# Linear attention and a squared-ReLU FFN: emitting each batch's attention beside the FFN block before it, with weights in memory of their own

One core of a Trainium2 chip. The metric is the device time of one execution in microseconds (us), the median of several runs; lower is better.

## The reference, cut to what matters

```python
# q, k, v: [8 batches, 8 heads, 576 rows, 64], float32
kv  = einsum('bhsd,bhse->bhde', k, v)
out = einsum('bhsd,bhde->bhse', q, kv)
rms = sqrt(mean(out * out, axis=-1, keepdims=True) + 1e-06)
x   = (out / rms * g_norm)  -> tokens [4608, 512]
h   = maximum(x @ w_in, 0.0)          # w_in  [512, 2048]
y   = h * h @ w_out                   # w_out [2048, 512]
```

Attention of a batch gives 576 tokens. The FFN runs over blocks of 512 tokens, nine of them. So FFN block i needs attention batches 0 to i, and none later.

## The kernel before

The whole of attention comes first, in pools that are then released; then the weights are loaded into pools that take over that memory; then the FFN runs, in pools that take over the memory of the load buffers. Matmuls are in bf16. A scheduler orders the instructions of each engine when the kernel is built; on the chip each engine takes them in that fixed order.

```python
    def attention():
        apool = ctx.enter_context(tc.tile_pool(name="attn_sb", bufs=6))
        ppool = ctx.enter_context(tc.tile_pool(name="attn_ps", bufs=1, space=PSUM))
        for b in range(B):
            kv_ps_list = [ppool.tile([P, P], dt, tag=f"kv_ps{p}") for p in range(NP)]   # 4 banks
            for ci, (ss, sl) in enumerate(s_chunks):       # 5 chunks: 4 of 128 rows, 1 of 64
                # ... load kkf, vvf; cast to kk (ScalarE), vv (VectorE)
                for p in range(NP):
                    nc.tensor.matmul(kv_ps_list[p], lhsT=kpair, rhs=vpair, ...)
            # ... kv_sb = kv_ps * block-diagonal mask (VectorE)
            for ci, (ss, sl) in enumerate(s_chunks):
                # ... load qqf, cast qq; 4 transposes qT_ps, copy qT (VectorE), 4 matmuls o_ps
                # ... sq = o_ps^2 (ScalarE), sum ss (VectorE), sqrt (ScalarE), 1/x and o_sb (VectorE)
                # ... 4 transposes oT_ps, xT = oT_ps * g (VectorE)
    # ... attention(), its pools released
    wpool = ctx.enter_context(tc.tile_pool(name="w", bufs=1))
    with tc.tile_pool(name="w_tmp", bufs=2) as wtmp:
        # 4 loads of w_in, 16 of w_out, each cast to bf16 by VectorE
    fpool  = ctx.enter_context(tc.tile_pool(name="ffn_sb", bufs=2))
    fppool = ctx.enter_context(tc.tile_pool(name="ffn_ps", bufs=4, space=PSUM))
    for t0 in range(0, n_tokens, T):                       # T = 512
        for nf in range(FC):
            # 4 matmuls into hps; h2 = relu(hps) (ScalarE); h2 = h2 * h2 (VectorE)
        for mt in range(T // P):
            # 16 matmuls into yps; ysb = yps (VectorE); store
```

Of the kernel before, what the change touches and what calls it, by code (L numbers as in the profile page):

```python
# [12 lines left out]
def kernel(  # L13
# [10 lines left out]
    nc = tc.nc  # L24
    P = 128
    B, H, S, D = q.shape
    d_model = H * D
    n_tokens = B * S
    d_ff = moe_w_in.shape[1]
    KC = d_model // P  # L30
    FC = d_ff // P
    dt = mybir.dt.float32
    AF = mybir.ActivationFunctionType
    ALU = mybir.AluOpType

    s_chunks = []
    s0 = 0
    while s0 < S:
        sl = min(P, S - s0)
# [2 lines left out]

    bf = mybir.dt.bfloat16
    HPP = P // D

    const = ctx.enter_context(tc.tile_pool(name="const", bufs=1))
    identity = const.tile([P, P], dt)
    make_identity(nc, identity)
    identity_bf = const.tile([P, P], bf)
    nc.vector.tensor_copy(out=identity_bf, in_=identity)  # L50
    bdm = const.tile([P, P], dt)
# [3 lines left out]
    g_perm = const.tile([P, 1], dt)  # L55
    g_part_ap = bass.AP(tensor=g_norm.tensor, offset=g_norm.offset,
                        ap=[[int(g_norm.ap[0][0]), D], [0, 1]])
    nc.sync.dma_start(out=g_perm[:D, :], in_=g_part_ap)
    nc.sync.dma_start(out=g_perm[D:, :], in_=g_part_ap)
    eps_sb = const.tile([P, 1], dt)  # L60
    nc.vector.memset(eps_sb, 1e-6)

    xT = const.tile([P, KC, n_tokens], bf)

    def attention():
        apool = ctx.enter_context(tc.tile_pool(name="attn_sb", bufs=6))
        ppool = ctx.enter_context(tc.tile_pool(name="attn_ps", bufs=1, space=bass.MemoryType.PSUM))
        NP = H // HPP
        ns = len(s_chunks)
        for b in range(B):  # L70
            kv_ps_list = [ppool.tile([P, P], dt, tag=f"kv_ps{p}", name=f"kv_ps{p}")
                          for p in range(NP)]
            for ci, (ss, sl) in enumerate(s_chunks):
                kkf = apool.tile([P, H, D], dt, tag="kkf")
                vvf = apool.tile([P, H, D], dt, tag="vvf")
                nc.sync.dma_start(out=kkf[:sl], in_=k[b, :, ss:ss + sl, :].rearrange("h s d -> s h d"))  # L76
                nc.sync.dma_start(out=vvf[:sl], in_=v[b, :, ss:ss + sl, :].rearrange("h s d -> s h d"))  # L77
                kk = apool.tile([P, H, D], bf, tag="kk")
                vv = apool.tile([P, H, D], bf, tag="vv")
                nc.scalar.activation(out=kk[:sl], in_=kkf[:sl], func=AF.Copy)  # L80
                nc.vector.tensor_copy(out=vv[:sl], in_=vvf[:sl])  # L81
                for p in range(NP):
                    kpair = kk[:sl, p * HPP:(p + 1) * HPP, :].rearrange("s h d -> s (h d)")
                    vpair = vv[:sl, p * HPP:(p + 1) * HPP, :].rearrange("s h d -> s (h d)")
                    nc.tensor.matmul(kv_ps_list[p], lhsT=kpair, rhs=vpair,  # L85
                                     start=(ci == 0), stop=(ci == ns - 1))
            kv_sb = apool.tile([P, NP, P], bf, tag="kv_sb")
            for p in range(NP):
                nc.vector.tensor_mul(out=kv_sb[:, p, :], in0=kv_ps_list[p], in1=bdm)

            for ci, (ss, sl) in enumerate(s_chunks):
                qqf = apool.tile([P, H, D], dt, tag="qqf")
                nc.sync.dma_start(out=qqf[:sl], in_=q[b, :, ss:ss + sl, :].rearrange("h s d -> s h d"))
                qq = apool.tile([P, H, D], bf, tag="qq")
                nc.scalar.activation(out=qq[:sl], in_=qqf[:sl], func=AF.Copy)  # L95
                o_ps = ppool.tile([P, NP, P], dt, tag="o_ps", bufs=2)
                qT_ps = ppool.tile([P, NP, P], bf, tag="qT_ps")
                for p in range(NP):
                    qpair = qq[:sl, p * HPP:(p + 1) * HPP, :].rearrange("s h d -> s (h d)")
                    nc.tensor.transpose(qT_ps[:, p, :sl], qpair, identity_bf[:sl, :sl])  # L100
                qT = apool.tile([P, NP, P], bf, tag="qT")
                nc.vector.tensor_copy(out=qT[:, :, :sl], in_=qT_ps[:, :, :sl])  # L102
                for p in range(NP):
                    nc.tensor.matmul(o_ps[:sl, p, :], lhsT=qT[:, p, :sl],  # L104
                                     rhs=kv_sb[:, p, :], start=True, stop=True)

                o_sb = apool.tile([P, NP, P], bf, tag="o_sb")
                sq = apool.tile([P, H, D], dt, tag="sqsb")
                ss_ = apool.tile([P, H], dt, tag="ss")
                nc.scalar.activation(out=sq[:sl], in_=o_ps[:sl], func=AF.Square)  # L110
                nc.vector.tensor_reduce(out=ss_[:sl], in_=sq[:sl],
                                        axis=mybir.AxisListType.X, op=ALU.add)
                nc.scalar.activation(out=ss_[:sl], in_=ss_[:sl], func=AF.Sqrt,
                                     scale=1.0 / D, bias=eps_sb[:sl])
                nc.vector.reciprocal(out=ss_[:sl], in_=ss_[:sl])
                sslice = ss_[:sl]
                rstd_bc = bass.AP(tensor=sslice.tensor, offset=sslice.offset,
                                  ap=[list(sslice.ap[0]), list(sslice.ap[1]), [0, D]])
                nc.vector.tensor_mul(out=o_sb[:sl], in0=o_ps[:sl], in1=rstd_bc)  # L119

                oT_ps = ppool.tile([P, NP, P], bf, tag="oT_ps")
                for p in range(NP):
                    nc.tensor.transpose(oT_ps[:, p, :sl], o_sb[:sl, p, :], identity_bf[:sl, :sl])  # L123
                nc.vector.tensor_scalar(  # L124
                    out=xT[:, :, b * S + ss: b * S + ss + sl],
                    in0=oT_ps[:, :, :sl], scalar1=g_perm, scalar2=None, op0=ALU.mult)

    with ExitStack() as actx:
        oc = ctx
        ctx = actx  # L130
        attention()
        ctx = oc

    wpool = ctx.enter_context(tc.tile_pool(name="w", bufs=1))
    w_in_sb = wpool.tile([P, KC, d_ff], bf)
    w_out_sb = wpool.tile([P, FC, d_model], bf)
    with tc.tile_pool(name="w_tmp", bufs=2) as wtmp:
        for kk in range(KC):
            t_in = wtmp.tile([P, d_ff], dt, tag="win")
            nc.sync.dma_start(out=t_in, in_=moe_w_in.rearrange(  # L140
                "(kc ki) n -> ki kc n", ki=P)[:, kk, :])
            nc.vector.tensor_copy(out=w_in_sb[:, kk, :], in_=t_in)
        for kk in range(FC):
            t_out = wtmp.tile([P, d_model], dt, tag="wout")
            nc.sync.dma_start(out=t_out, in_=moe_w_out.rearrange(
                "(fc fi) n -> fi fc n", fi=P)[:, kk, :])
            nc.vector.tensor_copy(out=w_out_sb[:, kk, :], in_=t_out)  # L147

    T = 512
    fpool = ctx.enter_context(tc.tile_pool(name="ffn_sb", bufs=2))  # L150
    fppool = ctx.enter_context(tc.tile_pool(name="ffn_ps", bufs=4, space=bass.MemoryType.PSUM))

    for t0 in range(0, n_tokens, T):
        h2 = fpool.tile([P, FC, T], bf, tag="h2")
        for nf in range(FC):
            hps = fppool.tile([P, T], dt, tag="hps")
            for kk in range(KC):
                nc.tensor.matmul(hps,  # L158
                                 lhsT=w_in_sb[:, kk, nf * P:(nf + 1) * P],
                                 rhs=xT[:, kk, t0:t0 + T],  # L160
                                 start=(kk == 0), stop=(kk == KC - 1))
            nc.scalar.activation(out=h2[:, nf, :], in_=hps, func=AF.Relu)  # L162
            nc.vector.tensor_mul(out=h2[:, nf, :], in0=h2[:, nf, :], in1=h2[:, nf, :])  # L163

        for mt in range(T // P):
            yps = fppool.tile([P, d_model], dt, tag="yps")
            for kk in range(FC):
                nc.tensor.matmul(yps,  # L168
                                 lhsT=h2[:, kk, mt * P:(mt + 1) * P],
                                 rhs=w_out_sb[:, kk, :],  # L170
                                 start=(kk == 0), stop=(kk == FC - 1))
            ysb = fpool.tile([P, d_model], dt, tag="ysb")
            nc.vector.tensor_copy(out=ysb, in_=yps)  # L173
            nc.sync.dma_start(out=out[t0 + mt * P: t0 + (mt + 1) * P, :], in_=ysb)


# [28 lines left out]
```

## Time and profile before

| | before |
|---|---|
| time | 445.55 us (444.17 to 446.51, 5 runs); 445.41 over all 16 runs |
| attention, until the first w_in load | 153.4 us |
| weights, until TensorE runs freely | 39.2 us |
| FFN | 248.0 us |
| TensorE / VectorE / ScalarE busy | 76 / 46 / 38% of the span |

The windows, chain and waits that tell the three stages apart stand in the prediction. Here is the strip of the page, 40 slices of 11.1 us each, a digit for tenths busy (DMA is the mean over the core's 16 DMA engines):

```profile
PE   1356656656566342069999999999999999999996
DMA  8999999999999185510201102011010110101101
```

DMA is full for the first 13 slices (attention), loads the weights in the next five and then does little; TensorE is half idle for 17 and then full. The two strips are complementary, and that is what the change is after.

Three rows of the instruction groups matter later (count, total busy us, mean ns of one; then the idle time ahead of them and its cause). These are three of the four kinds of attention matmul, each 128 columns wide:

```profile
L85 PE MATMUL kv_ps<-vv,kk 128*128 128x128 bf16 (+1 forms) x160 | 22.1, 301 | 30.4 <-DVE vv L81 30.3
L104 PE MATMUL o_ps<-kv_sb,qT 128*128 128x128 bf16 (+1 forms) x160 | 24.9, 311 | 8.3 <-DVE qT L102 8.3
L123 PE MATMUL oT_ps<-identity_bf,o_sb 128*128 128x128 bf16 (+1 forms) x160 | 22.6, 293 | 21.6 <-DVE o_sb L119 21.3
```

### The profile page before, as it was taken

The numbers are of one execution on the slowest core, as the hardware profiler recorded it, in microseconds if no ns is written. First come the engines' busy times: TensorE is split into PE (matmuls) and PEld (weight loads), VectorE is DVE, ScalarE is ACT, GpSimd is POOL, SyncE is SP. The second block draws the span as 40 slices with busy tenths as digits, with TensorE's granted clock in tenths as the row PEclk, the third lists the DMA queues.
The fourth block names the chain that finished last, engine by engine and source line by source line (L and its number), as shares of the span: only waits on it lengthen the run. The fifth ranks groups of instructions, "written<-read, shape, count | busy, mean of one in ns | idle before, by whom it ended". The sixth has DMA issues, their size and how long they took to land.

```text
span 444.4 us, 4875 instructions
## 1 busy us (share of the span) xinstructions
PE 338.8 (76%) x1792; PEld 173.3 (39%) x1792; DVE 205.0 (46%) x474; ACT 167.7 (38%) x306; POOL 1.1 (0%) x9
## 2 busy tenths in 40 slices
PE   1356656656566342069999999999999999999996
PEld 0244444444344210024444444444444444444442
DVE  0387786786777633233242332423324243242431
ACT  2465565565456300044160431604316053160530
POOL 0000000000000000000000000000000000000000
PEclk9999999999999999999999999999999999999999
DMA  8999999999999185510201102011010110101101
GB/s 154 205 210 205 203 209 205 208 204 200 200 214 144 32 364 170 150 39 9 87 0 49 47 20 76 0 49 47 25 71 0 49 48 25 71 0 49 47 25 71
DMA packets 120759, 46.45 MB, mean 105 GB/s; under 512 B 113568, under 2 KB 113568, under 8 KB 120224
## 3 DMA queue, kind: packets, MB, share of 16 engines
q1 hardware_dynamic: 120736, 46.15, 48.2%
q8 instruction: 14, 0.23, 0.2%
q14 instruction: 9, 0.07, 0.1%
HBM read 36.70 MB, written 9.44 MB: 104 GB/s over the span
## 4 chain that ended last, share of the span: by engine, by line
PE 65%; DMA 14%; DVE 12%; ACT 3%; SPq 3%; issue 2%; ACTq 0%
PE yps L168 28%; PE hps L158 28%; DMA qqf<-in_q_dram 7%; DMA t_out<-in_moe_w_out_dram 4%; PE oT_ps L123 4%; DVE o_sb L119 3%; DMA t_in<-in_moe_w_in_dram 3%; DVE qT L102 2%; PE qT_ps L100 2%; DVE xT L124 2%; ACT qq L95 2%; PE o_ps L104 2%; SPq L77 1%; SPq L76 1%; PE kv_ps L85 1%
## 5 line engine op out<-in xcount | busy, mean ns | idle before, releaser
L162 ACT ACTIVATE h<-hps 128x512 bf16<-128x512 f32 x144 | 85.7, 597 | 190.3 <-PE hps L158 149.8
L158 PE MATMUL hps<-xT,w_in_sb 128*128 128x512 bf16 x576 | 132.5, 391 | 32.1 <-ACT h L162 22.5
L168 PE MATMUL yps<-w_out_sb,h 128*128 128x512 bf16 x576 | 125.8, 379 | 0.0
L158 PEld LDWEIGHTS <-w_in_sb 128*128 128x128 bf16 x576 | 57.2, 100 | 105.8 <-issue 35.7
L163 DVE TENSOR_TENSOR h<-h 128x512 bf16<-128x512 bf16 x144 | 61.2, 425 | 67.3 <-ACT h L162 67.1
L168 PEld LDWEIGHTS <-h 128*128 128x128 bf16 x576 | 56.4, 98 | 67.9
L173 DVE COPY ysb<-yps 128x512 f32<-128x512 f32 x36 | 24.9, 692 | 96.2 <-PE yps L168 96.2
L85 PE MATMUL kv_ps<-vv,kk 128*128 128x128 bf16 (+1 forms) x160 | 22.1, 301 | 30.4 <-DVE vv L81 30.3
L123 PE MATMUL oT_ps<-identity_bf,o_sb 128*128 128x128 bf16 (+1 forms) x160 | 22.6, 293 | 21.6 <-DVE o_sb L119 21.3
L104 PE MATMUL o_ps<-kv_sb,qT 128*128 128x128 bf16 (+1 forms) x160 | 24.9, 311 | 8.3 <-DVE qT L102 8.3
L80 ACT ACTIVATE kk<-kkf 128x512 bf16<-128x512 f32 (+1 forms) x40 | 24.0, 619 | 17.5 <-DMA kkf<-in_k_dram 17.5
L85 PEld LDWEIGHTS <-kk 128*128 128x128 bf16 (+1 forms) x160 | 16.8, 131 | 34.8 <-issue 21.3
L100 PE MATMUL qT_ps<-identity_bf,qq 128*128 128x128 bf16 (+1 forms) x160 | 23.2, 297 | 9.4 <-ACT qq L95 9.4
L95 ACT ACTIVATE qq<-qqf 128x512 bf16<-128x512 f32 (+1 forms) x40 | 24.9, 623 | 13.8 <-DMA qqf<-in_q_dram 13.8
L110 ACT ACTIVATE sq<-o_ps 128x512 f32<-128x512 f32 (+1 forms) x40 | 23.7, 592 | 12.8 <-PE o_ps L104 12.8
L123 PEld LDWEIGHTS <-o_sb 128*128 128x128 bf16 (+1 forms) x160 | 12.9, 128 | 30.8 <-DVE o_sb L119 30.0
L81 DVE CAST vv<-vvf 128x512 bf16<-128x512 f32 (+1 forms) x40 | 15.3, 402 | 15.4 <-DMA vvf<-in_v_dram 15.4
L102 DVE COPY qT<-qT_ps 128x512 bf16<-128x512 bf16 (+1 forms) x40 | 15.7, 393 | 14.0 <-PE qT_ps L100 14.0
L124 DVE TENSOR_SCALAR xT<-oT_ps,g_perm 128x512 bf16<-128x512 bf16 (+1 forms) x40 | 18.3, 457 | 7.8 <-PE oT_ps L123 5.0
L104 PEld LDWEIGHTS <-qT 128*128 128x128 bf16 (+1 forms) x160 | 16.2, 144 | 14.1 <-DVE qT L102 12.5
L100 PEld LDWEIGHTS <-qq 128*128 128x128 bf16 (+1 forms) x160 | 15.8, 140 | 13.5 <-ACT qq L95 13.2
L147 DVE CAST w_out_sb<-t_out 128x512 bf16<-128x512 f32 x16 | 6.7, 426 | 17.0 <-DMA t_out<-in_moe_w_out_dram 17.0
(175 smaller groups left out, 90.2 us busy)
## 6 DMA issues: line engine op xcount, KB each, us to landing
out_dram<-ysb SPq DMA_DIRECT2D x36, 256.0 KB, 2.0
kkf<-in_k_dram SPq DMA_DIRECT2D x32, 256.0 KB, 5.1
vvf<-in_v_dram SPq DMA_DIRECT2D x32, 256.0 KB, 5.2
qqf<-in_q_dram SPq DMA_DIRECT2D x32, 256.0 KB, 5.4
t_in<-in_moe_w_in_dram SPq DMA_DIRECT2D x4, 1024.0 KB, 5.1
t_out<-in_moe_w_out_dram SPq DMA_DIRECT2D x16, 256.0 KB, 2.7
kkf<-in_k_dram SPq DMA_DIRECT2D x8, 128.0 KB, 4.9
vvf<-in_v_dram SPq DMA_DIRECT2D x8, 128.0 KB, 4.6
```

The lines of the kernel that those rows point to most:

```text
L85: nc.tensor.matmul(kv_ps_list[p], lhsT=kpair, rhs=vpair, start=(ci == 0), stop=(ci == ns - 1))
L95: nc.scalar.activation(out=qq[:sl], in_=qqf[:sl], func=AF.Copy)
L100: nc.tensor.transpose(qT_ps[:, p, :sl], qpair, identity_bf[:sl, :sl])
L102: nc.vector.tensor_copy(out=qT[:, :, :sl], in_=qT_ps[:, :, :sl])
L104: nc.tensor.matmul(o_ps[:sl, p, :], lhsT=qT[:, p, :sl], rhs=kv_sb[:, p, :], start=True, stop=True)
L123: nc.tensor.transpose(oT_ps[:, p, :sl], o_sb[:sl, p, :], identity_bf[:sl, :sl])
L124: nc.vector.tensor_scalar(out=xT[:, :, b * S + ss: b * S + ss + sl], in0=oT_ps[:, :, :sl], scalar1=g_perm, scalar2=None, op0=ALU.mult)
L158: nc.tensor.matmul(hps, lhsT=w_in_sb[:, kk, nf * P:(nf + 1) * P], rhs=xT[:, kk, t0:t0 + T], start=(kk == 0), stop=(kk == KC - 1))
L162: nc.scalar.activation(out=h2[:, nf, :], in_=hps, func=AF.Relu)
L163: nc.vector.tensor_mul(out=h2[:, nf, :], in0=h2[:, nf, :], in1=h2[:, nf, :])
L168: nc.tensor.matmul(yps, lhsT=h2[:, kk, mt * P:(mt + 1) * P], rhs=w_out_sb[:, kk, :], start=(kk == 0), stop=(kk == FC - 1))
L173: nc.vector.tensor_copy(out=ysb, in_=yps)
```

## The change

The intent: let the FFN's matmuls run while DMA brings the next batch, and let the weights come in early. The weights and their load buffers get memory of their own; the four kv_ps tiles are packed into one PSUM bank; FFN tiles share one tag of 3 buffers, so that everything fits into eight banks together; attention buffers go from 6 to 4; and the program emits attention of batch i+1 just ahead of FFN block i. The FFN's h2 and ysb move into the attention pool, where ysb gets 4 buffers in place of 2. Otherwise the bodies are the same but for the lines shown.

```diff
-    (attention() over all batches, pools released; wpool, wtmp, fpool, fppool after it)
+    w_in_sb = const.tile([P, KC, d_ff], bf)
+    w_out_sb = const.tile([P, FC, d_model], bf)
+    wtmp = ctx.enter_context(tc.tile_pool(name="w_tmp", bufs=2))
+    apool = ctx.enter_context(tc.tile_pool(name="attn_sb", bufs=4))
+    ppool = ctx.enter_context(tc.tile_pool(name="ps", bufs=1, space=bass.MemoryType.PSUM))
     ...
-            hps = fppool.tile([P, T], dt, tag="hps")
+            hps = ppool.tile([P, T], dt, tag="fps", name="hps", bufs=3)
     ...
-            kv_ps_list = [ppool.tile([P, P], dt, tag=f"kv_ps{p}", name=f"kv_ps{p}")
-                          for p in range(NP)]
+        kv_ps = ppool.tile([P, NP, P], dt, tag="kv_ps", name="kv_ps")
     ...
-                    nc.tensor.matmul(kv_ps_list[p], lhsT=kpair, rhs=vpair,
-                                     start=(ci == 0), stop=(ci == ns - 1))
+                nc.tensor.matmul(kv_ps[:, p, :], lhsT=kpair, rhs=vpair,
+                                 start=(ci == 0 and p == 0), stop=(ci == ns - 1),
+                                 skip_group_check=True)
     ...
+    attn_batch(0)
+    load_weights()
+    for i in range(n_tokens // T):
+        if i + 1 < B:
+            attn_batch(i + 1)
+        ffn_block(i * T)
```

More of the change, by code (lines that the diff above doesn't have):

```diff
@@ L44 @@
     HPP = P // D
+    NP = H // HPP
+    ns = len(s_chunks)
     const = ctx.enter_context(tc.tile_pool(name="const", bufs=1))
@@ L63 @@
     xT = const.tile([P, KC, n_tokens], bf)
-    def attention():
-        apool = ctx.enter_context(tc.tile_pool(name="attn_sb", bufs=6))
-        ppool = ctx.enter_context(tc.tile_pool(name="attn_ps", bufs=1, space=bass.MemoryType.PSUM))
-        NP = H // HPP
-        ns = len(s_chunks)
-        for b in range(B):
-            kv_ps_list = [ppool.tile([P, P], dt, tag=f"kv_ps{p}", name=f"kv_ps{p}")
-                          for p in range(NP)]
-            for ci, (ss, sl) in enumerate(s_chunks):
-                kkf = apool.tile([P, H, D], dt, tag="kkf")
-                vvf = apool.tile([P, H, D], dt, tag="vvf")
-                nc.sync.dma_start(out=kkf[:sl], in_=k[b, :, ss:ss + sl, :].rearrange("h s d -> s h d"))
-                nc.sync.dma_start(out=vvf[:sl], in_=v[b, :, ss:ss + sl, :].rearrange("h s d -> s h d"))
-                kk = apool.tile([P, H, D], bf, tag="kk")
-                vv = apool.tile([P, H, D], bf, tag="vv")
-                nc.scalar.activation(out=kk[:sl], in_=kkf[:sl], func=AF.Copy)
-                nc.vector.tensor_copy(out=vv[:sl], in_=vvf[:sl])
-                for p in range(NP):
-                    kpair = kk[:sl, p * HPP:(p + 1) * HPP, :].rearrange("s h d -> s (h d)")
-                    vpair = vv[:sl, p * HPP:(p + 1) * HPP, :].rearrange("s h d -> s (h d)")
-                    nc.tensor.matmul(kv_ps_list[p], lhsT=kpair, rhs=vpair,
-                                     start=(ci == 0), stop=(ci == ns - 1))
-            kv_sb = apool.tile([P, NP, P], bf, tag="kv_sb")
-            for p in range(NP):
-                nc.vector.tensor_mul(out=kv_sb[:, p, :], in0=kv_ps_list[p], in1=bdm)
-            for ci, (ss, sl) in enumerate(s_chunks):
-                qqf = apool.tile([P, H, D], dt, tag="qqf")
-                nc.sync.dma_start(out=qqf[:sl], in_=q[b, :, ss:ss + sl, :].rearrange("h s d -> s h d"))
-                qq = apool.tile([P, H, D], bf, tag="qq")
-                nc.scalar.activation(out=qq[:sl], in_=qqf[:sl], func=AF.Copy)
-                o_ps = ppool.tile([P, NP, P], dt, tag="o_ps", bufs=2)
-                qT_ps = ppool.tile([P, NP, P], bf, tag="qT_ps")
-                for p in range(NP):
-                    qpair = qq[:sl, p * HPP:(p + 1) * HPP, :].rearrange("s h d -> s (h d)")
-                    nc.tensor.transpose(qT_ps[:, p, :sl], qpair, identity_bf[:sl, :sl])
-                qT = apool.tile([P, NP, P], bf, tag="qT")
-                nc.vector.tensor_copy(out=qT[:, :, :sl], in_=qT_ps[:, :, :sl])
-                for p in range(NP):
-                    nc.tensor.matmul(o_ps[:sl, p, :], lhsT=qT[:, p, :sl],
-                                     rhs=kv_sb[:, p, :], start=True, stop=True)
-                o_sb = apool.tile([P, NP, P], bf, tag="o_sb")
-                sq = apool.tile([P, H, D], dt, tag="sqsb")
-                ss_ = apool.tile([P, H], dt, tag="ss")
-                nc.scalar.activation(out=sq[:sl], in_=o_ps[:sl], func=AF.Square)
-                nc.vector.tensor_reduce(out=ss_[:sl], in_=sq[:sl],
-                                        axis=mybir.AxisListType.X, op=ALU.add)
-                nc.scalar.activation(out=ss_[:sl], in_=ss_[:sl], func=AF.Sqrt,
-                                     scale=1.0 / D, bias=eps_sb[:sl])
-                nc.vector.reciprocal(out=ss_[:sl], in_=ss_[:sl])
-                sslice = ss_[:sl]
-                rstd_bc = bass.AP(tensor=sslice.tensor, offset=sslice.offset,
-                                  ap=[list(sslice.ap[0]), list(sslice.ap[1]), [0, D]])
-                nc.vector.tensor_mul(out=o_sb[:sl], in0=o_ps[:sl], in1=rstd_bc)
-                oT_ps = ppool.tile([P, NP, P], bf, tag="oT_ps")
-                for p in range(NP):
-                    nc.tensor.transpose(oT_ps[:, p, :sl], o_sb[:sl, p, :], identity_bf[:sl, :sl])
-                nc.vector.tensor_scalar(
-                    out=xT[:, :, b * S + ss: b * S + ss + sl],
-                    in0=oT_ps[:, :, :sl], scalar1=g_perm, scalar2=None, op0=ALU.mult)
@@ L128, with load_weights @@
-    with ExitStack() as actx:
-        oc = ctx
-        ctx = actx
-        attention()
-        ctx = oc
-    wpool = ctx.enter_context(tc.tile_pool(name="w", bufs=1))
-    w_in_sb = wpool.tile([P, KC, d_ff], bf)
-    w_out_sb = wpool.tile([P, FC, d_model], bf)
-    with tc.tile_pool(name="w_tmp", bufs=2) as wtmp:
+    w_in_sb = const.tile([P, KC, d_ff], bf)
+    w_out_sb = const.tile([P, FC, d_model], bf)
+    wtmp = ctx.enter_context(tc.tile_pool(name="w_tmp", bufs=2))
+    def load_weights():
@@ L147, with ffn_block @@
             nc.vector.tensor_copy(out=w_out_sb[:, kk, :], in_=t_out)
+    apool = ctx.enter_context(tc.tile_pool(name="attn_sb", bufs=4))
+    ppool = ctx.enter_context(tc.tile_pool(name="ps", bufs=1, space=bass.MemoryType.PSUM))
     T = 512
-    fpool = ctx.enter_context(tc.tile_pool(name="ffn_sb", bufs=2))
-    fppool = ctx.enter_context(tc.tile_pool(name="ffn_ps", bufs=4, space=bass.MemoryType.PSUM))
-    for t0 in range(0, n_tokens, T):
-        h2 = fpool.tile([P, FC, T], bf, tag="h2")
+    def ffn_block(t0):
+        h2 = apool.tile([P, FC, T], bf, tag="h2", name="h2", bufs=2)
         for nf in range(FC):
-            hps = fppool.tile([P, T], dt, tag="hps")
+            hps = ppool.tile([P, T], dt, tag="fps", name="hps", bufs=3)
             for kk in range(KC):
@@ L165 @@
         for mt in range(T // P):
-            yps = fppool.tile([P, d_model], dt, tag="yps")
+            yps = ppool.tile([P, d_model], dt, tag="fps", name="yps", bufs=3)
             for kk in range(FC):
@@ L171, with attn_batch @@
                                  start=(kk == 0), stop=(kk == FC - 1))
-            ysb = fpool.tile([P, d_model], dt, tag="ysb")
+            ysb = apool.tile([P, d_model], dt, tag="ysb", name="ysb")
             nc.vector.tensor_copy(out=ysb, in_=yps)
             nc.sync.dma_start(out=out[t0 + mt * P: t0 + (mt + 1) * P, :], in_=ysb)
+    def attn_batch(b):
+        kv_ps = ppool.tile([P, NP, P], dt, tag="kv_ps", name="kv_ps")
+        for ci, (ss, sl) in enumerate(s_chunks):
+            kkf = apool.tile([P, H, D], dt, tag="kkf")
+            vvf = apool.tile([P, H, D], dt, tag="vvf")
+            nc.sync.dma_start(out=kkf[:sl], in_=k[b, :, ss:ss + sl, :].rearrange("h s d -> s h d"))
+            nc.sync.dma_start(out=vvf[:sl], in_=v[b, :, ss:ss + sl, :].rearrange("h s d -> s h d"))
+            kk = apool.tile([P, H, D], bf, tag="kk")
+            vv = apool.tile([P, H, D], bf, tag="vv")
+            nc.scalar.activation(out=kk[:sl], in_=kkf[:sl], func=AF.Copy)
+            nc.vector.tensor_copy(out=vv[:sl], in_=vvf[:sl])
+            for p in range(NP):
+                kpair = kk[:sl, p * HPP:(p + 1) * HPP, :].rearrange("s h d -> s (h d)")
+                vpair = vv[:sl, p * HPP:(p + 1) * HPP, :].rearrange("s h d -> s (h d)")
+                nc.tensor.matmul(kv_ps[:, p, :], lhsT=kpair, rhs=vpair,
+                                 start=(ci == 0 and p == 0), stop=(ci == ns - 1),
+                                 skip_group_check=True)
+        kv_sb = apool.tile([P, NP, P], bf, tag="kv_sb")
+        for p in range(NP):
+            nc.vector.tensor_mul(out=kv_sb[:, p, :], in0=kv_ps[:, p, :], in1=bdm)
+        for ci, (ss, sl) in enumerate(s_chunks):
+            qqf = apool.tile([P, H, D], dt, tag="qqf")
+            nc.sync.dma_start(out=qqf[:sl], in_=q[b, :, ss:ss + sl, :].rearrange("h s d -> s h d"))
+            qq = apool.tile([P, H, D], bf, tag="qq")
+            nc.scalar.activation(out=qq[:sl], in_=qqf[:sl], func=AF.Copy)
+            o_ps = ppool.tile([P, NP, P], dt, tag="o_ps", bufs=2)
+            qT_ps = ppool.tile([P, NP, P], bf, tag="qT_ps")
+            for p in range(NP):
+                qpair = qq[:sl, p * HPP:(p + 1) * HPP, :].rearrange("s h d -> s (h d)")
+                nc.tensor.transpose(qT_ps[:, p, :sl], qpair, identity_bf[:sl, :sl])
+            qT = apool.tile([P, NP, P], bf, tag="qT")
+            nc.vector.tensor_copy(out=qT[:, :, :sl], in_=qT_ps[:, :, :sl])
+            for p in range(NP):
+                nc.tensor.matmul(o_ps[:sl, p, :], lhsT=qT[:, p, :sl],
+                                 rhs=kv_sb[:, p, :], start=True, stop=True)
+            o_sb = apool.tile([P, NP, P], bf, tag="o_sb")
+            sq = apool.tile([P, H, D], dt, tag="sqsb")
+            ss_ = apool.tile([P, H], dt, tag="ss")
+            nc.scalar.activation(out=sq[:sl], in_=o_ps[:sl], func=AF.Square)
+            nc.vector.tensor_reduce(out=ss_[:sl], in_=sq[:sl],
+                                    axis=mybir.AxisListType.X, op=ALU.add)
+            nc.scalar.activation(out=ss_[:sl], in_=ss_[:sl], func=AF.Sqrt,
+                                 scale=1.0 / D, bias=eps_sb[:sl])
+            nc.vector.reciprocal(out=ss_[:sl], in_=ss_[:sl])
+            sslice = ss_[:sl]
+            rstd_bc = bass.AP(tensor=sslice.tensor, offset=sslice.offset,
+                              ap=[list(sslice.ap[0]), list(sslice.ap[1]), [0, D]])
+            nc.vector.tensor_mul(out=o_sb[:sl], in0=o_ps[:sl], in1=rstd_bc)
+            oT_ps = ppool.tile([P, NP, P], bf, tag="oT_ps")
+            for p in range(NP):
+                nc.tensor.transpose(oT_ps[:, p, :sl], o_sb[:sl, p, :], identity_bf[:sl, :sl])
+            nc.vector.tensor_scalar(
+                out=xT[:, :, b * S + ss: b * S + ss + sl],
+                in0=oT_ps[:, :, :sl], scalar1=g_perm, scalar2=None, op0=ALU.mult)
```

## The prediction

> **What bounds the kernel now.** I first cut the span into its stages with a table of windows (start:end, length, busy time of each engine with the number of instructions, granted clock, mean number of transfers, GB/s).
>
> ```profile
> 0.00:153.40 153.40, 83.31 (x640) 59.70 (x640) 107.34 (x274) 82.00 (x162) 1.09 (x9) 1.00 1.08 185
> 153.40:192.60 39.20, 7.53 (x16) 1.88 (x17) 11.57 (x21) 0.64 (x2) 0.00 (x0) 1.00 0.61 214
> 192.60:440.60 248.00, 247.99 (x1136) 111.73 (x1135) 85.38 (x179) 85.03 (x143) 0.00 (x0) 1.00 0.10 38
> 440.60:444.40 3.80, 0.00 (x0) 0.00 (x0) 0.69 (x1) 0.00 (x0) 0.00 (x0) 0.91 0.18 69
> ```
>
> Three stages with three limits. Attention: 153.4 us with DMA saturated and no compute engine over 70% busy. Loading the FFN weights: 39.2 us in which TensorE issues 16 matmuls. The FFN: 248.0 us, TensorE always busy, DMA a tenth busy.
>
> The chain that ended last, in order of time (start, length, piece), tells what each stage waits for.
>
> ```profile
> 81.00 5.02 DMA qqf<-in_q_dram
> 86.04 0.64 ACT qq L95
> ...
> 153.42 6.93 DMA t_in<-in_moe_w_in_dram
> ...
> 191.37 0.44 DVE w_out_sb L147
> 191.96 0.61 ACT h L162
> 192.60 13.17 PE hps L158 x48
> 205.77 13.81 PE yps L168 x64
> 219.58 13.81 PE hps L158 x64
> ```
>
> In attention it enters each batch through a q load, every 17 us. In the FFN it is pure TensorE: 64 matmuls in 13.81 us, 216 ns each, no gap; a block of 512 tokens is 27.62 us. Between them is a serial wait, and the waits view shows why it is so long:
>
> ```profile
> ACT h L162 <- DVE w_out_sb L147: 40.5, 1, 40.5
> PE hps L158 <- ACT h L162: 22.5, 1, 22.5
> SPq L140 <- DVE o_sb L119: 9.8, 1, 9.8
> ```
>
> The first Relu waits for the last cast of w_out, though it does not use w_out: I take it that its tile lies in the memory that the load buffers had, and so waits for their last reader. So TensorE stands 22.5 us with its four PSUM tiles full. The first weight load in turn waits for the last o_sb of attention: the weights too lie where attention buffers had been.
>
> **What the Trainium skill says.** "TensorE: Matmul & The Clock Gate", Part 1, gives start-to-start 106.7/426.7 ns at N=128/512 while the array is cold and 55.6/215.7 ns once it is warm after some 3.4 us of sustained work. The trace agrees at N=512: the first matmuls after the 22.5 us hole start 0.425 us apart, later ones 0.216. The weight loads of the kv matmuls (L85, N=128) start about 0.105 us apart, so attention runs cold; beside the FFN it should run warm. "PSUM — Partial Sum Buffer", The four PSUM rules, says that a first matmul clears the written bits of its whole bank, so that groups sharing a bank may set the flag only on the first one issued there. The new packed kv_ps does that. It is a matter of correctness; no trace of before shows it. "DMA: Bandwidth & Descriptors", Specifications, puts line rate at pieces of 512 B or more: the q, k, v loads go in 256-byte pieces, and this trace moves 205 GB/s in attention against 437 GB/s while w_in loads.
>
> **The change part by part.** No arithmetic and no byte is added or removed: the same 1792 matmuls, 28.3 MB of q, k, v and 8.4 MB of weights. Weights and their load buffers get memory of their own; kv_ps shrinks from four banks to one, so that attention and FFN fit in the eight banks together (FFN tiles 3 instead of 8); attention buffers go from 6 to 4; attention of batch i+1 is emitted ahead of FFN block i. I read the order in which each engine will execute. The two are really interleaved: in block 4, for instance, TensorE does the kv groups, 7 FFN matmuls, 4 of o_ps, 4 of qT, 3 FFN matmuls, and so on. The second products (yps) of blocks 3 to 6 stand as 64 in a row. Blocks 7 and 8 have no attention beside them.
>
> (1) Start until FFN block 1 begins. Batch 0 runs as before: its last chunk was done at 33.1 us in the old trace. The first two w_in loads are now issued near 19 us, behind the q loads; their casts (1.23 us each) fall into DVE's chain for batch 0. The other two loads wait for those casts, and take 5.1 us from issue to landing: I put the last w_in cast at 40 us. Of the 64 hps matmuls 9 can be done by then; 55 x 0.216 = 11.9 us, plus some cold ones and two kv groups: done at about 55. The yps matmuls need all 16 pieces of w_out. They still go two at a time, each pair costing about 3.25 us in the old trace (casts at 171.09, 174.19, 177.44), and four of them pass before 41 us, the next four at the pace of the squares ahead of them on DVE; I get the last cast at 66. Then the remaining yps, three PSUM copies and kv_sb of batch 1 until 70. The chain of batch 1 then has almost no FFN left to hide it, because FFN block 1 needs tokens up to 1023, which are chunk 3 of batch 1: in the old trace chunk 3 came 10.8 us after the first transpose of a batch. Block 1 starts at about **81 us**.
>
> (2) Blocks 1 to 6, with batches 2 to 7: FFN 27.6 us; 80 attention matmuls. Cold they would be 80 x 0.107 = 8.6 us; the skill's warm spacing would make 4.5, and between the two, since each group waits for its operand and shows a weight load, I take 6.9 us (an estimate). Then stalls: DVE per batch has 13.1 us of attention (the window of 68 to 85 us) and per FFN block 16 x 0.425 + 4 x 0.692 = 9.6 us, 22.7 in a block of some 37, so not the bound on average. But the chain from kv_sb to the last xT falls into the hps half: about 12 us of attention and some ten squares, 16 to 17 us of DVE, where TensorE has about 46 FFN matmuls (9.9 us) and 15 attention groups (5 us). So DVE is locally the slower one, and I allow 3 us a block. Sum 37.5 x 6 = **225 us**.
>
> (3) Blocks 7 and 8: 2 x 27.6 = **55 us**. (4) Tail after the last matmul as before: **4 us**. Sum 81 + 225 + 55 + 4 = 365 us of span; the timed runs are about 1 us longer: **366 us**.
>
> What no longer sets the end is the 17 us per batch of DMA: 3.54 MB of a batch at 205 GB/s is 17.3 us, and the 1.05 MB of an output block some 4 more, 22 us inside a block of 37.
>
> **Rivals.** (A) The fixed order bites. Each engine takes its instructions in order; a Relu behind a square root that waits for a DVE sum holds up the FFN's PSUM tiles, of which there are now 3 instead of 8. For it: in attention alone TensorE already stood waiting for o_sb (21.3 us in total) and vv (30.3). Against: the order puts at least 4.3 us of TensorE work between o_ps of chunk 0 and its transposes, where the old chain took 3.7. If it costs 8 us a block in place of 3: 396 us. (B) The start is longer. The w_out loads share the one issuing queue with the k and v loads, at about 1.1 us of issue each, and their casts share DVE with the squares, so a pair can take 5 us instead of 3.25. Six pairs then cost 10 us more: 376. (C) A full hiding: attention at the warm spacing and stalls of 1 us only give 33.1 a block: 339. A start at 72 would bring it to 330. (D) DMA again: loads of the next batch stand behind output stores, which wait for yps. With 4 buffers for k, v and q, four of five chunks are fetched a block ahead, so that only late batches of q could arrive late; I see at most 2 us a block in it, 378. (E) No gain: it would need stalls of 16 us a block, all of the attention put back on the path. The interleaved order speaks against it; only a misordered wait between the engines could do it.
>
> **Range and chances.** A and B point up, C down, each worth 10 to 30 us. I predict 366 us, with 347 to 390 to hold it 8 times in 10. Faster by over 2% means under 436.6 us, and even A and B together (406) stay under it: 0.97. Within 2%: 0.02. Slower: 0.01.
>
> **What would show each step.** The page after should have TensorE busy from about 40 us to the end, with DMA at 5 to 7 tenths until some 300 us instead of 9 and then 1. The wait of h for w_out_sb over 40 us must be gone. The first hps of block 1 should start at 81 us give or take 6; the middle blocks should be 37.5 us apart from yps to yps, the last two 27.6. The matmul records of attention should become shorter than 293 to 311 ns, which shows the warm clock. If stalls are near 3 us a block, hps should wait for ACT h, and oT_ps for DVE o_sb, with DVE over 80% busy in the hps halves. The prediction is wrong if the blocks with attention take over 41 or under 34 us (step 2), or if the start differs by over 10 us (step 1).

## The result, and the profile after

The changed kernel takes **343.97 us** (342.23 to 345.10, 9 runs) against 445.41 us (443.04 to 446.56, 16 runs). The ratio is 0.7721, 95% interval 0.7706 to 0.7737. A ratio is the mean time of one kernel's fast runs over that of the other's of the same rounds, so not quite the ratio of the medians quoted. It is below the predicted range (347 to 390): the direction was right, and the gain was larger than foreseen.

The strip of the page of the changed kernel (slices of 8.6 us):

```profile
PE   0256699866999999999999999999999999999995
DMA  7994978999835789389478956880110020011011
```

TensorE is full from slice 10 on (counted from 0), and DMA works beside it until slice 26.

The windows of the changed kernel (columns as in the prediction: length, then busy us and count for PE, weight loads, DVE, ACT, POOL; clock, DMA, GB/s). The rows are the start up to the last w_in cast, the rest of FFN block 0, block 1, block 4 with the kv groups ahead of it, and the last two blocks:

```profile
0.00:39.30 39.30, 14.71 (x90) 8.46 (x90) 19.06 (x43) 12.89 (x22) 1.09 (x9) 1.00 0.93 227
39.30:81.66 42.36, 35.30 (x196) 16.59 (x196) 26.67 (x67) 19.52 (x37) 0.00 (x0) 0.95 0.91 216
81.66:119.26 37.60, 37.42 (x225) 18.05 (x225) 23.91 (x60) 20.34 (x39) 0.00 (x0) 0.92 0.69 135
185.20:218.20 33.00, 32.95 (x211) 16.61 (x209) 21.01 (x55) 17.89 (x36) 0.00 (x0) 1.00 0.84 179
283.83:339.10 55.27, 55.25 (x256) 24.85 (x254) 19.13 (x40) 19.12 (x32) 0.00 (x0) 1.00 0.10 39
```

FFN block 1 begins at 81.66 us. A block with attention beside it takes 33.0 us (block 1: 37.6), where the FFN alone takes 27.6. So a whole batch of attention costs 5.4 us of TensorE's time; before, it took 17 us of DMA's time on the path. From block 2 on (119.1 to 283.6 us) the waits view lists no wait of a TensorE matmul.

The timeline of the changed kernel in block 4 shows how (start, length of the piece up to the modelled end of its last matmul, count):

```profile
187.90 0.39 PE L144 MATMUL o_ps<-kv_sb,qT 128*128 128x128 bf16 x4
188.12 0.39 PE L140 MATMUL qT_ps<-identity_bf,qq 128*128 128x128 bf16 x4
188.34 0.81 PE L93 MATMUL hps<-xT,w_in_sb 128*128 128x512 bf16 x3
189.03 0.40 PE L144 MATMUL o_ps<-kv_sb,qT 128*128 128x128 bf16 x4
```

From one group of four to the next it is 0.22 us, so 55 ns a matmul, where the weight loads of attention before stood 0.105 us apart. (The clock column of the prediction reads 1.00 there all the same: the trace of the kernel before has no clock record earlier than 198 us. The run below with the emission order undone has one, and it shows 0.52 where attention runs alone.) The groups of the whole kernel agree: the mean record of the same three kinds of matmul has become shorter by 22 to 25%.

```profile
L124 PE MATMUL kv_ps<-vv,kk 128*128 128x128 bf16 (+1 forms) x160 | 14.4, 231 | 14.3 <-DVE vv L120 13.9
L144 PE MATMUL o_ps<-kv_sb,qT 128*128 128x128 bf16 (+1 forms) x160 | 17.1, 234 | 1.2 <-DVE qT L142 1.0
L163 PE MATMUL oT_ps<-identity_bf,o_sb 128*128 128x128 bf16 (+1 forms) x160 | 16.2, 229 | 7.9 <-DVE o_sb L159 7.9
```

The wait of 40.5 us of the first Relu for w_out is gone, and the wait of oT_ps for o_sb, 21.3 us before, is 7.9 us, all of it in batches 0 and 1 (4.8 us before 36 us, 3.1 us between 66 and 84).

### The profile page after: what moved, and what is told of

The parts are those of the page before. It is cut to its first block, busy times and chain, and to the rows that moved or that the text cites. A ratio compares the mean times of both kernels' runs of the same rounds, so it can differ in the third digit from the quotient of the medians.

```text
span 342.8 us, 4757 instructions
## 1 busy us (share of the span) xinstructions
PE 307.0 (90%) x1792; PEld 150.5 (44%) x1792; DVE 193.8 (57%) x474; ACT 159.5 (47%) x306; POOL 1.1 (0%) x9
## 4 chain that ended last, share of the span: by engine, by line
PE 78%; DMA 8%; DVE 7%; ACT 3%; SPq 2%; issue 1%
PE hps L93 36%; PE yps L102 32%; PE oT_ps L163 3%; DMA t_out<-in_moe_w_out_dram 3%; PE o_ps L144 3%; PE qT_ps L140 2%; DMA qqf<-in_q_dram 2%; PE kv_ps L124 2%; DMA kkf<-in_k_dram 1%; DMA t_in<-in_moe_w_in_dram 1%; DVE o_sb L159 1%; DVE w_in_sb L76 1%; ACT h L97 1%; DVE xT L164 1%; DVE ysb L107 1%
## 5 line engine op out<-in xcount | busy, mean ns | idle before, releaser
L93 PE MATMUL hps<-xT,w_in_sb 128*128 128x512 bf16 x576 | 142.4, 393 | 4.1 <-DVE w_in_sb L76 3.0
L102 PE MATMUL yps<-w_out_sb,h 128*128 128x512 bf16 x576 | 129.4, 379 | 1.6 <-DVE w_out_sb L81 1.1
L98 DVE TENSOR_TENSOR h<-h 128x512 bf16<-128x512 bf16 x144 | 58.2, 415 | 34.0 <-ACT h L97 32.5
L124 PE MATMUL kv_ps<-vv,kk 128*128 128x128 bf16 (+1 forms) x160 | 14.4, 231 | 14.3 <-DVE vv L120 13.9
L163 PE MATMUL oT_ps<-identity_bf,o_sb 128*128 128x128 bf16 (+1 forms) x160 | 16.2, 229 | 7.9 <-DVE o_sb L159 7.9
L124 PEld LDWEIGHTS <-kk 128*128 128x128 bf16 (+1 forms) x160 | 11.6, 102 | 20.6 <-ACT kk L119 10.1
L140 PE MATMUL qT_ps<-identity_bf,qq 128*128 128x128 bf16 (+1 forms) x160 | 16.4, 224 | 2.9 <-DVE qT L142 1.6
L144 PE MATMUL o_ps<-kv_sb,qT 128*128 128x128 bf16 (+1 forms) x160 | 17.1, 234 | 1.2 <-DVE qT L142 1.0
L144 PEld LDWEIGHTS <-qT 128*128 128x128 bf16 (+1 forms) x160 | 11.2, 107 | 8.8 <-DVE qT L142 5.9
L140 PEld LDWEIGHTS <-qq 128*128 128x128 bf16 (+1 forms) x160 | 11.0, 102 | 9.4 <-ACT qq L135 4.9
```

What stands on the lines that cost most here:

```text
L93: nc.tensor.matmul(hps, lhsT=w_in_sb[:, kk, nf * P:(nf + 1) * P], rhs=xT[:, kk, t0:t0 + T], start=(kk == 0), stop=(kk == KC - 1))
L98: nc.vector.tensor_mul(out=h2[:, nf, :], in0=h2[:, nf, :], in1=h2[:, nf, :])
L102: nc.tensor.matmul(yps, lhsT=h2[:, kk, mt * P:(mt + 1) * P], rhs=w_out_sb[:, kk, :], start=(kk == 0), stop=(kk == FC - 1))
L124: nc.tensor.matmul(kv_ps[:, p, :], lhsT=kpair, rhs=vpair, start=(ci == 0 and p == 0), stop=(ci == ns - 1), skip_group_check=True)
L140: nc.tensor.transpose(qT_ps[:, p, :sl], qpair, identity_bf[:sl, :sl])
L144: nc.tensor.matmul(o_ps[:sl, p, :], lhsT=qT[:, p, :sl], rhs=kv_sb[:, p, :], start=True, stop=True)
```

## The experiments

Theory: the gain has a part from the false waits of the weight stage and a larger part from running attention beside the FFN. My sum was too high because attention there costs only its warm array time. Rivals are stated with each run. All twelve kernels gave correct results; "after" is the changed kernel. The scheduler makes the order of instructions anew for each of them, so an edit can also shift work that it doesn't name.

**Memory alone.** The kernel before, with only the memory moved.

```diff
+    w_in_sb, w_out_sb in const; wtmp, apool (bufs=4), fpool opened ahead of attention()
     attention()        # as before, PSUM pools still one after the other
     (load weights); (FFN)
```

> The kernel before with memory of their own for the weights, the load buffers and the FFN tiles, and 4 attention buffers, but attention still wholly ahead of the FFN. My theory: the gain of the change has two parts, the false waits of the weight stage and the interleaving. Here only the first shows: w_in starts about 10 us earlier, the first Relu no longer waits 22.5 us for w_out; about 411 us (some 34 of the 101 us). Rival 1, the false waits were the bulk of it: under 385. Rival 2, the weights only move into a DMA-bound stage and come out as long: 435 or more.

Measured: 416.2 us, ratio 0.9351 (0.9319 to 0.9382), so 28 us of the 101. The first hps starts at 154.6 us, right after attention, and the Relus follow; but then the second products wait for w_out, which still comes two pieces at a time. The chain of this kernel:

```profile
170.73 2.78 DMA t_out<-in_moe_w_out_dram
173.54 0.44 DVE w_out_sb L148
173.99 2.72 DMA t_out<-in_moe_w_out_dram
```

So the false waits are the smaller part, some 28 us; the theory's 34 was a little too much. Taking attention buffers from 6 to 4 did little harm: attention ends at 154.5 us, where it ended at 153.3.

**The emission order undone.** Memory and PSUM as in the change, but all eight batches emitted ahead of all FFN blocks.

```diff
-    attn_batch(0); load_weights()
-    for i in range(9): attn_batch(i + 1); ffn_block(i * T)
+    for i in range(8):
+        attn_batch(i)
+        if i == 0: load_weights()
+    for i in range(9): ffn_block(i * T)
```

> The changed kernel with all eight attention batches emitted ahead of all FFN blocks (weights still after batch 0); memory and PSUM as in the change. Its order shows FFN blocks 0 and 1 woven in, then dense attention with no FFN beside it. Theory, the gain of the steady part is FFN work beside attention: blocks 2 to 8 stand behind batches 3 to 7 at 17 us each, so about 118 + 80 + 7 x 27.6 + 4 = 395 us. Rival, shared pools alone suffice whatever the emission order: within 3% of 344.

Measured: 399.5 us, ratio 0.8985 (0.8963 to 0.9008). The windows of this kernel after its block 1:

```profile
118.00:199.80 81.80, 51.28 (x382) 34.90 (x379) 63.49 (x161) 44.34 (x92) 0.00 (x0) 0.52 0.95 188
199.80:394.00 194.20, 194.20 (x902) 87.85 (x899) 67.38 (x141) 66.97 (x112) 0.00 (x0) 1.00 0.10 38
```

Batches 3 to 7 take 81.8 us by themselves with DMA full, then seven FFN blocks 194 us. Shared pools do not suffice: 55 us of the gain come from the emission order. It is not undone wholly: FFN blocks 0 and 1 are still woven with batches 1 and 2 here, so this is what the order is worth to the later blocks. The clock column, 0.52 and then 1.00, is the record of attention running cold when it runs alone.

**A second set of o_ps matmuls.** This measures the price of an attention matmul beside the FFN.

```diff
                 nc.tensor.matmul(o_ps[:sl, p, :], lhsT=qT[:, p, :sl], rhs=kv_sb[:, p, :], start=True, stop=True)
+                nc.tensor.matmul(o_ps[:sl, p, :], lhsT=qT[:, p, :sl], rhs=kv_sb[:, p, :], start=True, stop=True)
```

> The changed kernel with every o_ps matmul done twice into the same place (same result): 160 more matmuls of N=128, 120 of them beside the FFN. Theory, beside the FFN the array is warm and such a matmul costs its 56 ns and nothing else: 120 x 0.056 = 6.7 us, plus up to 2 us for batches 0 and 1, so 351 to 353 us, ratio to before about 0.79. Rival, what I predicted with (86 ns each with its share of waits): 355 to 357. Rival, cold at 107 ns: 358 or more.

Measured: 352.83 us, ratio 0.7951 (0.7923 to 0.7979). The starts of yps halves in the chain give the length of a block. First the kernel after, blocks 3, 5 and 6 (the half of block 4 is cut into pieces there); then this kernel, blocks 3, 4 and 5:

```profile
171.09 13.83 PE yps L102 x64
...
237.06 13.83 PE yps L102 x64
270.02 13.81 PE yps L102 x64
```

```profile
177.67 13.83 PE yps L102 x64
211.86 13.83 PE yps L102 x64
246.07 13.83 PE yps L102 x64
```

After: (270.02 - 171.09) / 3 = 32.98 us a block. Doubled: (246.07 - 177.67) / 2 = 34.20. The 1.22 us buy 20 matmuls, 61 ns each. The total time fits the theory (351 to 353). The 86 ns I had predicted with would have made the block 34.7, the cold 107 ns 35.1; both are ruled out. What I expected too low was the start, where block 1 comes at 85.6 us in place of 81.7.

**More work for VectorE.** In block 4 VectorE is nearly full in the hps half, and I had charged 3 us a block for that. So I gave it more.

```diff
             nc.vector.tensor_mul(out=o_sb[:sl], in0=o_ps[:sl], in1=rstd_bc)
+            ss2 = apool.tile([P, H], dt, tag="ss2")
+            nc.vector.tensor_reduce(out=ss2[:sl], in_=sq[:sl], axis=X, op=ALU.add)   # unused
```

> The changed kernel with a second, unused sum over sq on DVE for each chunk, off the chain: 5 x 0.67 = 3.35 us more of DVE a batch. In the changed kernel DVE was 94 to 98% busy in the hps half of block 4 and 24% in the yps half. Theory A, DVE is just at its limit in the hps half, so that the extra work comes out of TensorE's time: 2 to 3.3 us a block, 356 to 364 us. Theory B, the squares can slip into the yps half and there is slack: under 350 us.

Measured: 345.18 us, ratio 0.7770 (0.7750 to 0.7790), 1.2 us more than the changed kernel by the medians, some 2 by the ratios. In the profiles block 1 starts 1.4 us later (83.05 us); from the first hps of block 4 to that of block 5 it is 33.06 us in both. The hps and yps halves of block 4, first after, then this kernel (DVE is the third busy time):

```profile
186.39:203.99 17.60, 17.60 (x122) 8.98 (x123) 16.73 (x46) 15.03 (x31) 0.00 (x0) 1.00 0.90 172
203.99:217.80 13.81, 13.81 (x65) 6.27 (x64) 3.33 (x7) 1.71 (x4) 0.00 (x0) 1.00 0.75 183
```

```profile
186.73:204.33 17.60, 17.60 (x121) 9.01 (x120) 17.04 (x44) 15.40 (x32) 0.00 (x0) 1.00 0.92 174
204.33:218.70 14.37, 14.37 (x77) 6.89 (x76) 5.79 (x14) 1.42 (x3) 0.00 (x0) 1.00 0.79 187
```

The hps half lasts 17.60 us in both, with VectorE at 95% and 97%, and TensorE has no gap. The extra work moved to the yps half (the second window is 0.56 us longer and holds a little of the next block's start, so its DVE time is not exactly comparable). My theory A, that VectorE at 95% is at its limit, fell; theory B held. VectorE's deferrable work is the squares: an hps tile is freed by its Relu on ScalarE, and the square is needed only by yps. Of the 16 squares of block 4, 14 start in the hps half after, 9 in this kernel. So it is the order made anew that moved them; what more VectorE work would do in the order of the changed kernel was not run. That order also put more FFN matmuls between the groups of a chunk (12 in one place where there were 3 or 4).

**Two PSUM tiles for the FFN in place of three.**

```diff
-            hps = ppool.tile([P, T], dt, tag="fps", name="hps", bufs=3)
+            hps = ppool.tile([P, T], dt, tag="fps", name="hps", bufs=2)      # and so for yps
```

> The changed kernel with 2 instead of 3 PSUM tiles for the FFN. Theory, three tiles give just the room that the Relus need when ACT is 86% busy in the hps half; with two, each Relu must come within one group of 0.86 us: 2 to 5 us more a block, 356 to 375 us. Rival, PSUM tiles were never a limit, so that my warning of 3 instead of 8 was idle: under 348.

Measured: 344.32 us, ratio 0.7755 (0.7717 to 0.7793), the interval touching that of the changed kernel. The theory fell: the PSUM tiles are no limit, with the order made for two.

**The FFN block emitted ahead of the next batch.**

```diff
     for i in range(n_tokens // T):
+        ffn_block(i * T)
         if i + 1 < B:
             attn_batch(i + 1)
-        ffn_block(i * T)
```

> The changed kernel with FFN block i emitted ahead of attention batch i+1. Same instructions and buffers, another fixed order: attention groups stand in clumps between the yps and the hps with little FFN work between them. Theory, how small the waits are in the changed kernel is owed to the order: here 4 to 8 us more a block, 370 to 395 us. Rival, the engines are loose enough that the order matters little: under 352.

Measured: 380.43 us, ratio 0.8553 (0.8517 to 0.8589), 36 us more than after, with the same instructions and buffers. The order that comes out puts the attention groups in clumps between yps and hps, and the waits of attention's own chain are exposed again in every block. The waits over 130 to 280 us, four blocks of 37.5 us (total, times, longest):

```profile
PE oT_ps L163 <- DVE o_sb L159: 5.6, 8, 1.1
PE qT_ps L140 <- DVE qT L142: 4.1, 6, 0.7
```

With small ones they are 11.6 us, 2.9 a block, where the view of the changed kernel lists none; and in each of these blocks the granted clock is 0.50 for about 3.4 us, which at half speed can cost up to 1.7. Together that would account for the 4.5 us by which the block is longer. So the waits for o_sb that rival A named are real, and the emission order is what avoids them; a Relu holding up PSUM tiles, A's other half, does not show among the waits.

**The start.** Four kernels tried to shorten the 81.7 us until block 1, since the rest is TensorE nearly without gaps.

```diff
-            t_out = wtmp.tile([P, d_model], dt, tag="wout")
+            t_out = wtmp.tile([P, d_model], dt, tag="wout", bufs=8)
```

> The changed kernel with 8 instead of 2 load buffers for w_out. Theory, the start (81.7 us until FFN block 1) is held up by w_out coming two pieces at a time behind the squares on DVE; with 8 the last cast comes some 8 us earlier: about 335 us. Rival, the start is set by the loads of batch 1 and its unhidden chain: 341 or more.

Measured: 342.61 us, ratio 0.7712 (0.7683 to 0.7741): no gain that stands out. The last cast of w_out came at 51.0 us instead of 65.7, and yps ran without a hole from 53.5 to 68.2 us, yet block 1 began at 79.6. The chain of this kernel shows what is there instead:

```profile
68.24 0.24 PE qT_ps L140 x4
...
78.40 0.62 PE oT_ps L163 x4
79.05 0.49 DVE xT L164
79.58 0.58 PE hps L93
```

That is batch 1, bare. Its loads were issued at 45.8 to 62 us, behind all of w_out. A wait was removed and the next stood behind it: the rival was right.

The second one added to this the weight loads on another issuing queue (`nc.gpsimd.dma_start` in place of `nc.sync.dma_start` for t_in and t_out):

> As with 8 load buffers, and the weight loads issued from GpSimd instead of from the queue that issues q, k and v. Its order weaves batch 1 fully into FFN block 0. Theory, weights no longer wait behind q, and batch 1 is hidden: block 1 starts some 10 to 15 us earlier, 327 to 334 us. Rival, DMA bandwidth of the first 60 us is the limit (7.1 MB of two batches at 205 GB/s and 8.4 MB at 437 are 54 us): no better than with 8 buffers alone, 335 to 344.

Measured: 342.70 us, ratio 0.7717 (0.7691 to 0.7742). Batch 1 was indeed hidden, and TensorE's gaps from the first hps on come to under 0.5 us, but that hps came at 47.4 us instead of 31.8. This fits the rival, by which the same bytes must come first in either order; it was not tested further.

The third, with 8 load buffers and the old queue, put `load_weights()` ahead of `attn_batch(0)` and emitted attention two batches ahead:

> Weights emitted ahead of batch 0, 8 load buffers, and attention two batches ahead of the FFN instead of one. Theory, the unhidden chain of batch 1 goes, and only batch 0 stands ahead of the FFN: about 330 us. Rival, the weights delay batch 0 by what they take (20 us at 437 GB/s) and nothing is won: 340 or more.

Measured: 349.16 us, ratio 0.7857 (0.7832 to 0.7883); the first hps starts at 53.9 us. Its rival's number was right too.

The fourth has 7 load buffers for w_out and loads k and v in larger pieces, two rows a partition:

```diff
-            kkf = apool.tile([P, H, D], dt, tag="kkf")
-            nc.sync.dma_start(out=kkf[:sl], in_=k[b, :, ss:ss + sl, :].rearrange("h s d -> s h d"))
+            kkf = apool.tile([P, H, 2 * D], dt, tag="kkf", bufs=3)
+            nc.sync.dma_start(out=kkf[:96], in_=k[b, :, r0:r0 + 192, :].rearrange("h (s j) d -> s h (j d)", j=2))
             # v likewise; 3 loads a batch; two casts and 8 kv matmuls for each
```

> Extra w_out buffers (7), and k and v loaded as two neighbouring rows a partition: 512-byte pieces instead of 256, three loads of 192 rows a batch instead of five of up to 128, 24 kv matmuls a batch instead of 20. Theory, the start is held by what DMA must bring for batches 0 and 1 at some 205 GB/s: k and v of a batch come in 5.5 instead of 11.5 us, so block 1 starts near 69 us instead of 80, and about 332 us in all. Rival, the start is held by the chains of casts and transposes: 340 or more.

Measured: 338.02 us, ratio 0.7596 (0.7575 to 0.7618). It gained 4.6 us on the kernel with 8 load buffers, but not for my reason. The DMA view of this kernel over 5 to 12 us, when almost only k and v are moving:

```profile
DMA packets 3001, 1.51 MB, mean 215 GB/s; under 512 B 58, under 2 KB 3001, under 8 KB 3001
```

The pieces are 512 bytes and the rate is 215 GB/s; in the same window of the changed kernel 256-byte pieces moved 222. The loads are no faster. What differs is the order that came out: batch 1 is now woven more fully into the yps of block 0, and block 1 starts at 76.7 us. That the new order caused the gain is an inference from this; I did not separate it.

Two more built on it: attention two batches ahead (`attn_batch(1)` after the weights, then `attn_batch(i + 2)` in the loop), and with that six rows a partition, one load of k and one of v a batch.

> As the one before with attention emitted two batches ahead. Its order differs little in the first block. Theory, nothing is left to hide, the same within 1%. Rival, a batch of reserve hides what remains of the chain of batch 1: 4 us or more below the other.

> As the kernel two batches ahead, but k and v loaded with six neighbouring rows a partition: 1536-byte pieces, one load of k and one of v a batch. With 512-byte pieces the loads still moved only 215 GB/s, as with 256. Theory, the rate depends on the piece and still grows above 512 bytes: over 300 GB/s in the first 8 us, block 1 starts near 70 us, about 330 us in all. Rival, the rate does not depend on the piece, but on the strided rows of these tensors: 215 GB/s again and 334 us or more.

Measured: 335.67 us, ratio 0.7549 (0.7522 to 0.7576), and 336.03 us, ratio 0.7551 (0.7530 to 0.7572). The first beats both kernels, by 24.5% and some 2.2%; by 2 us, less than the 4 that I had named, it is ahead of the kernel one batch ahead, with intervals that just touch. With 1536-byte pieces the rate over 5.3 to 9 us was 224 GB/s. So the rate did not depend on the piece between 256 and 1536 bytes, while the weight loads, mostly w_out in pieces of 2 KB, moved 368 GB/s over 34 to 46 us in the kernel with 8 load buffers. Why the k and v loads stay at six tenths of that is left open: strided rows and a step between 1536 bytes and 2 KB both remain.

## Why the prediction was wrong in size

By its own steps:

1. *Start until block 1, 81 us.* Right: 81.66 us. The pieces were near as well: last w_in cast at 39.3 us (predicted 40), first yps at 54.1 (55), last w_out cast at 66 (66), then the bare chain of batch 1.
2. *Blocks 1 to 6, 225 us.* **This is the step that failed**: 283.83 - 81.66 = 202.2 us. Both terms that I put on top of the FFN's 27.6 us were too large. "80 attention matmuls ... I take 6.9 us": they cost 20 groups x 0.22 = 4.4 us, as the spacing in the timeline shows and the doubled o_ps confirms to 6 ns a matmul (61 ns each in place of my 86). I had quoted the warm spacing of the clock gate and worked out the 4.5 us, and then left it for a value halfway to cold without a row that asked for it. "I allow 3 us a block" of waits: 33.0 - 27.6 - 4.4 leaves 1.0; in the starts of block 4 it is spread over pauses between groups, the longest 0.21 us, and the waits view lists none of a matmul in blocks 2 to 6. The observation behind it was sound, VectorE is 95% busy in that half, but what TensorE needed from it was not late. VectorE was full and still no bound: with more work and another order the block is as long as before, because squares can go into the yps half. The two terms together are 2.5 + 2.0 = 4.5 us over six blocks, 27 us; block 1, 4.6 us longer than the others, takes some back. The granted clock was 0.50 from 77.7 to 87.9 us, over the bare end of batch 1's chain and the first 6.2 us of block 1, which makes about 3.1 of the 4.6; its window also holds 14 attention matmuls more than that of block 4, 0.8 us; the rest is not accounted for. 27 - 4.6 is the 22 us by which the sum was high.
3. *Blocks 7 and 8, 55 us.* 55.3 us. *Tail, 4 us.* 3.7 us. The timed run is 1.9 us above the span of its profile, not 1.

Of the rivals, C (full hiding: 33.1 us a block, 339 us) is what happened, almost to the number of the block. A's waits for o_sb were no threat in this order, and a real one in another (380 us). B did not occur. D: the waits for q and k on ScalarE in blocks 3 to 6 made no gap in TensorE. The range was too high because I gave its lower side only to C, and weighted three rivals that point up.

Where the gain comes from, by the runs: separate memory for the weights and the FFN tiles alone gives 28 us; together with the change's PSUM layout, the early weights and the two FFN blocks woven in through them it is 45 us in all (445 to 400), and the emission order gives the other 55 (400 to 344).

## What to carry to other kernels

Where one stage is full on DMA and the next on TensorE, try running them beside each other: here the price of the first was then little more than its array time at the spacing of a warm array (5.4 us a batch, 4.4 of them array time, in place of 17), not its length when it runs bare. Before charging for a nearly full engine, ask which of its work can be late; a share of 95% busy with deferrable work in it cost TensorE no wait that the view lists. When instructions are woven by a scheduler, the emission order is a parameter as strong as any buffer count: the same instructions gave 344, 380 and 400 us.

## What the Trainium skill lacked or had wrong

- "TensorE: Matmul & The Clock Gate", Part 2, Back-to-back issue gap, gives a sustained 81 ns at N=128 and 131 ns at N=512 for pairs of weight load and matmul. Here such pairs run at 55 ns (groups of four 0.22 us apart) and 216 ns (64 in 13.81 us), which is the page's own warm formula, called isolated there.
- The same page, Part 4, has transposes at about 275 ns in a kernel's context, with the clock gate not opening for them. Between FFN matmuls the record of one transpose qT_ps is 219 ns (median of the changed kernel; 314 in the kernel before), and four of them started 0.22 us ahead of what followed, 55 ns each: woven into other work they run warm. Whether transposes alone would open the gate no run shows.
- "DMA: Bandwidth & Descriptors", Specifications, sets the least transfer for line rate at 512 B. The strided k and v loads moved 222, 215 and 224 GB/s with pieces of 256, 512 and 1536 bytes; the weights, in pieces of 2 KB and more, 368 GB/s. So 512 B was not enough here; whether a larger piece would be, or the strided rows decide, the runs do not show.
